# The passes of two matmul layers issued in turn, one by one instead of three by three

## The chip, the cores and the metric

The kernel runs on one core of a Trainium2 chip. The metric is the device time of one execution in microseconds (us), median over several runs. The core's engines are TensorE (PE, with its weight loads shown as PEld), VectorE (DVE), ScalarE (ACT), GpSimd (POOL) and SyncE (SP), which issues the transfers. Matmul results go to PSUM, eight banks of 128 partitions by 2 KB, where they are added up; ScalarE and VectorE read them out.

## The reference

The computation is an attention over channels followed by a two-layer network with the exact GELU, for 4 batches of 6080 tokens with 256 channels:

```python
qn = q / (norm(q, axis=1) + 1e-6); kn = k / (norm(k, axis=1) + 1e-6)
a = softmax(kn.transpose(0, 2, 1) @ qn / tau)      # 256 x 256 per batch
x = (v @ a).reshape(24320, 256)
h = x @ w_in                                       # 256 -> 2048
g = 0.5 * h * (1 + erf(h / sqrt(2)))
out = g @ w_out                                    # 2048 -> 256
```

## The kernel before, in words

The attention matrix is folded into the first layer's weights, so per batch one pair of weight matrices is left: tokens times 256x2048, GELU, times 2048x256. Precision is kept by splitting every operand into a high and a low part; a product of two operands is then three matmul passes (high by high, high by low, low by high) that add up in one PSUM bank.

The tokens of a batch are cut into 6 pairs of blocks (two blocks of 512 tokens each, the last pair of 480), the 2048 hidden channels into 8 slices. One slice of one pair is called a **unit** here; there are 4 x 6 x 8 = 192. In all but the first pair a unit's first layer is computed as a Strassen-like scheme of seven **products** (`first_products`, called P0 to P6 here), each of three passes (L458, L459, L460, called p1, p2, p3). They go into three banks. Bank *one* takes P0, P2, P4 and P6 in turn, added up: between them the partial sum is read out, after P0 and P2 by a copy on ScalarE (`kept`, L491), after P4 by an addition on VectorE (`added`, L496, which also follows P3 and P5). So P2 can't begin before the copy after P0 is done, nor P4 before the copy after P2, nor P6 before the addition after P4. Four blocks come out; each goes through GELU twice on ScalarE (`gh`, rounded, L466, and `g`, L467) and a subtraction on VectorE (`gl`, L468). The first pair uses eight plain products per unit instead.

The second layer of a unit is eight **groups** (`second_products`, called G0 to G7 here), each of three passes (L541, L542, L543, called s1, s2, s3; s1 and s3 read `gh`, s2 reads `gl`) into one of four other banks, which add up over the eight units of a pair. G0 and G1 read the first block made, G2 and G3 the last one made (out of P6). At a pair's end the four banks are copied out (L547 on ScalarE, L549 on VectorE).

`second_products` is a generator. The loop over the units runs the second layer one unit behind the first: while the products of a unit are written, the groups of the unit before are drawn in between, one group after each product, and the rest (G6's partner G7) at the unit's end. So TensorE gets three passes of a product, three of a group, and so on; a unit is 45 passes. Between units stand bursts of the next batch's scores (L191, L193) and, at a batch's end, the products that make the next batch's weights (L376 to L378).

The written order is not the last word: the framework that builds the program lists each engine's instructions itself, by its own estimate of when operands will be there, and keeps to the written order where it sees no reason to depart from it. Each engine then works through its list in order.

Of the kernel before, what the change touches and what calls it, by code (L numbers as in the profile page):

```python
# [60 lines left out]
def channel_attention_gelu_ffn(ctx, tc, qk, kqt, vt, tau, w_in, w_out, out):  # L61
# [38 lines left out]
    state = {}  # L100
# [3 lines left out]
    @contextmanager  # L104
    def behind(*names):
        with ExitStack() as stack:
            for name in names:
                stack.enter_context(tc.issue_after(marks[name].ins))
            yield
# [243 lines left out]
    def w_slot(g, i):  # L353
        if i != A21:
            return whs[g][:, i], wls[g][:, i]
        if g // 2 not in w21:
            w21[g // 2] = [pv.tile([P, 2, 2, P], F32R, name=f"v{x}{T2 + g // 2}") for x in "hl"]
        return [t[:, g % 2] for t in w21[g // 2]]
# [76 lines left out]
    def v_split(b, p, i):  # L435
        n = PAIRS[p][1]
        x = v_blocks(b, p)
        src = {B11: x[0, 0], B21: x[1, 0], B22: x[1, 1]}.get(i)
        if (b, p, i) == (0, 0, B12):
            src = x[0, 1]  # L440
        if src is None:
            src = vts[b, p][i - T1][:, :n]
        hi = pv.tile([P, NT], F32R, name=f"vh{i}")
        lo = pv.tile([P, NT], F32R, name=f"vl{i}")
        nc.scalar.copy(out=hi[:, :n], in_=src)
        nc.vector.tensor_tensor(out=lo[:, :n], in0=src, in1=f32(hi[:, :n]), op=ALU.subtract)
        vops[b, p, i] = hi, lo
# [5 lines left out]
    def product(b, p, u, a, v, ps, start, stop):  # L453
        n = PAIRS[p][1]
        g, q = divmod(u, 2)
        hi, lo = vops[b, p, v]
        wh, wl = (t[:, q] for t in w_slot(g, a))
        nc.tensor.matmul(ps[:, :n], wh, hi[:, :n], start=start, stop=False, skip_group_check=True)  # L458
        nc.tensor.matmul(ps[:, :n], wh, lo[:, :n], start=False, stop=False, skip_group_check=True)  # L459
        marks["product"] = nc.tensor.matmul(ps[:, :n], wl, hi[:, :n], start=False, stop=stop, skip_group_check=True)  # L460

    def gelu(src, n):
# [65 lines left out]
    def second_products(b, p, u, blocks):  # L528

        t0, n = PAIRS[p]  # L530
        wo = wos.pop((b, p, u))
        for j in range(2):
            for i in (1, 0):
                gh, gl = blocks[i, j]
                for c in range(NCT):
                    if u == 0 and i == 1:
                        po[j, c] = ps_o.tile([P, NT], F32, name="po")
                    o = po[j, c][:, :n]
                    cs = slice(c * P, (c + 1) * P)
                    first, last = u == 0 and i == 1, u == NU - 1 and i == 0  # L540
                    nc.tensor.matmul(o, wo[:, 0, i, cs], gh[:, :n], start=first, stop=False)  # L541
                    nc.tensor.matmul(o, wo[:, 0, i, cs], gl[:, :n], start=False, stop=False)  # L542
                    nc.tensor.matmul(o, wo[:, 1, i, cs], gh[:, :n], start=False, stop=last)  # L543
                    if last:
                        if c == 0:
                            osb = pg.tile([P, NCT, NT], F32, name="osb", bufs=2)
                            nc.scalar.copy(out=osb[:, 0, :n], in_=o)  # L547
                        else:
                            nc.vector.tensor_copy(out=osb[:, 1, :n], in_=o)  # L549
                            t = b * N + t0 + j * n  # L550
                            dst = out[:, t:t + n].rearrange("(t p) n -> p t n", p=P)
                            step = 1 if (b, p) == (B - 1, NP - 1) else NCT
                            for h in range(0, NCT, step):
                                nc.sync.dma_start(out=dst[:, h:h + step], in_=osb[:, h:h + step, :n])
                    yield
# [151 lines left out]
            w_group(b + 1, (w - 42) // 2)  # L707

    steps = [(b, p, u) for b in range(B) for p in range(NP) for u in range(NU)]
    second = iter(())  # L710
    for b, p, u in steps:
        pair = (b, p + 1) if p + 1 < NP else (b + 1, 0)
        products = plain_products if (b, p) == (0, 0) else first_products
        for i, _ in enumerate(products(b, p, u)):
            next(second, None)
            if u == NU - 1 and pair[0] < B and i < 6:
                v_split(*pair, ORDER[i][1])
        if u == NU - 1 and pair[0] < B:
            v_split(*pair, ORDER[6][1])
        for _ in second:  # L720
            pass
        if (b, p) == (0, 0):
            for _ in range(paces[u] if u < len(paces) else 0):
                with behind(*(["gelu"] if u == 0 else [])):
                    narrow_unit()
                if units:
                    load_unit()
        extras(b, p, u)
        second = second_products(b, p, u, state.pop("blocks"))
    for _ in second:  # L730
        pass

# [27 lines left out]
```

## Time and profile before

| what | value |
| --- | --- |
| median of 3 runs | 2187.51 us (2186.54 to 2188.09) |
| the profiled execution's own time | 2186.54 us |
| span of its instructions | 2184.8 us |
| TensorE busy | 2173.9 us |
| ScalarE busy | 1433.4 us (66%) |
| VectorE busy | 1391.2 us (64%) |

TensorE's busy time counts overlapping matmuls once; a matmul's recorded duration (0.39 us for 512 columns) runs into the next one's, so that the pace is read from the distance of two starts. The profiled execution is 1.74 us longer than its span and 0.97 us under the median.

### The profile page before, as it was taken

What the parts mean: (1) busy time and instruction counts of PE and PEld (TensorE: products, weight loads), DVE (VectorE), ACT (ScalarE), POOL (GpSimd) and SP (SyncE); (2) the same over time, 40 slices, a digit from 0 to 9 for tenths busy, and PEclk for the clock granted to TensorE, in tenths of its full rate; (3) what the DMA queues carried; (4) which work ended last, traced back from release to release, by engine and by line L of the source; (5) the groups of instructions that cost most, each with busy time, mean ns of one, the idle gap of its engine ahead of it and who ended that gap; (6) DMA issues with size and microseconds to landing.
All of it is one profiled execution on the core that took longest, in us unless ns stands there. A gap on an engine that the chain in (4) does not pass through costs nothing.

```text
span 2184.8 us, 26184 instructions
## 1 busy us (share of the span) xinstructions
PE 2173.9 (100%) x9664; PEld 1794.0 (82%) x9664; DVE 1391.2 (64%) x2179; ACT 1433.4 (66%) x2595; POOL 1.3 (0%) x8
## 2 busy tenths in 40 slices
PE   8999999999999999999999999999999999999999
PEld 7788888888888888888888888888888888888888
DVE  6995767656677575675667757657467555555554
ACT  6666666667566676676765666767576566666665
POOL 0000000000000000000000000000000000000000
PEclk9999999999999999999999999999999999999999
DMA  9552544422343343542323335343132122121121
GB/s 381 195 207 104 174 135 158 160 87 87 106 144 106 121 168 116 174 157 64 106 97 133 116 116 174 134 155 126 49 114 97 58 87 72 64 97 66 68 78 47
DMA packets 77056, 267.52 MB, mean 122 GB/s; under 512 B 7680, under 2 KB 9728, under 8 KB 74880
## 3 DMA queue, kind: packets, MB, share of 16 engines
q1 hardware_dynamic: 76928, 265.84, 35.3%
q8 instruction: 76, 1.25, 0.2%
q14 instruction: 52, 0.43, 0.1%
HBM read 232.52 MB, written 33.29 MB: 122 GB/s over the span
## 4 chain that ended last, share of the span: by engine, by line
PE 98%; DVE 1%; DMA 0%; ACT 0%; issue 0%; SPq 0%; ACTq 0%; DVEq 0%
PE po L543 16%; PE po L541 16%; PE po L542 16%; PE ph L460 14%; PE ph L459 14%; PE ph L458 14%; PE ph L191 3%; PE ph L149 2%; PE ph L193 1%; PE ph L378 1%; PE ph L376 1%; PE ph L377 1%; DMA raw<-qk 0%; DVE nt L243 0%; PE po L172 0%
## 5 line engine op out<-in xcount | busy, mean ns | idle before, releaser
L468 DVE TENSOR_TENSOR gl<-g,gh 128x512 fp32r<-128x512 f32 (+1 forms) x768 | 522.1, 682 | 145.9 <-ACT g L467 142.1
L543 PE MATMUL po<-gh,wo 128*128 128x512 f32 (+1 forms) x1536 | 605.4, 394 | 0.0
L541 PE MATMUL po<-gh,wo 128*128 128x512 f32 (+1 forms) x1536 | 599.3, 390 | 1.0 <-ACT gh L466 1.0
L542 PE MATMUL po<-gl,wo 128*128 128x512 f32 (+1 forms) x1536 | 596.0, 388 | 0.0
L496 DVE TENSOR_TENSOR h<-ph,p 128x512 f32<-128x512 f32 (+1 forms) x368 | 251.7, 684 | 534.2 <-PE ph L460 438.9
L460 PE MATMUL ph<-vh,wl 128*128 128x512 f32 (+1 forms) x1336 | 523.0, 391 | 0.0
L459 PE MATMUL ph<-vl,wh 128*128 128x512 f32 (+1 forms) x1336 | 521.7, 391 | 0.0
L458 PE MATMUL ph<-vh,wh 128*128 128x512 f32 (+1 forms) x1336 | 520.7, 390 | 0.2 <-ACT wh L362 0.2
L466 ACT ACTIVATE gh<-h 128x512 fp32r<-128x512 f32 (+1 forms) x552 | 345.1, 625 | 243.1 <-DVE h L496 238.4
L491 ACT COPY p<-ph 128x512 f32<-128x512 f32 (+1 forms) x368 | 213.3, 583 | 263.2 <-PE ph L460 262.9
L542 PEld LDWEIGHTS po<-gl,wo 128*128 128x128 f32 x1536 | 288.5, 188 | 63.9
L541 PEld LDWEIGHTS po<-gh,wo 128*128 128x128 f32 x1536 | 288.5, 188 | 62.6 <-ACT gh L466 1.5
L543 PEld LDWEIGHTS po<-gh,wo 128*128 128x128 f32 x1536 | 288.5, 188 | 61.3
L467 ACT ACTIVATE g<-h 128x512 f32<-128x512 f32 (+1 forms) x552 | 337.4, 611 | 0.0
L459 PEld LDWEIGHTS ph<-vl,wh 128*128 128x128 f32 x1336 | 251.3, 188 | 56.6
L458 PEld LDWEIGHTS ph<-vh,wh 128*128 128x128 f32 x1336 | 251.2, 188 | 54.0 <-DVE h L496 3.1
L460 PEld LDWEIGHTS ph<-vh,wl 128*128 128x128 f32 x1336 | 251.1, 188 | 50.6
L491 ACT COPY u<-ph 128x512 f32<-128x512 f32 (+1 forms) x184 | 106.7, 580 | 111.8 <-PE ph L460 111.8
L466 ACT ACTIVATE gh<-ph 128x512 fp32r<-128x512 f32 (+1 forms) x216 | 125.1, 579 | 23.6 <-PE ph L460 19.4
L467 ACT ACTIVATE g<-ph 128x512 f32<-128x512 f32 (+1 forms) x216 | 126.4, 586 | 1.6 <-DVE gl L468 1.5
L496 DVE TENSOR_TENSOR h<-ph,u 128x512 f32<-128x512 f32 (+1 forms) x184 | 125.4, 681 | 2.7
L209 ACT ACTIVATE kqc<-kqc 128x1024 f32<-128x1024 f32 x72 | 76.4, 1061 | 35.6 <-DMA kqc<-kqt 35.1
(135 smaller groups left out, 1351.4 us busy)
## 6 DMA issues: line engine op xcount, KB each, us to landing
wo<-keep_out SPq DMA_DIRECT2D x184, 512.0 KB, 3.3
raw<-qk SPq DMA_DIRECT2D x95, 512.0 KB, 4.2
kqc<-kqt SPq DMA_DIRECT2D x72, 512.0 KB, 4.4
v_raw<-vt SPq DMA_DIRECT2D x20, 1024.0 KB, 5.6
out<-osb SPq DMA_DIRECT2D x40, 512.0 KB, 3.4
win<-keep_in SPq DMA_DIRECT2D x12, 1024.0 KB, 4.8
keep_in<-win SPq DMA_DIRECT2D x4, 1024.0 KB, 4.6
keep_out<-wo SPq DMA_DIRECT2D x8, 512.0 KB, 3.8
```

The source lines that it names most:

```text
L209: nc.scalar.activation(out=x, in_=x, func=AF.Square, accum_out=state["nsum"][:, t, c:c + 1])
L458: nc.tensor.matmul(ps[:, :n], wh, hi[:, :n], start=start, stop=False, skip_group_check=True)
L459: nc.tensor.matmul(ps[:, :n], wh, lo[:, :n], start=False, stop=False, skip_group_check=True)
L460: marks["product"] = nc.tensor.matmul(ps[:, :n], wl, hi[:, :n], start=False, stop=stop, skip_group_check=True)
L466: nc.scalar.activation(out=gh[:, :n], in_=src, func=AF.Gelu)
L467: marks["gelu"] = nc.scalar.activation(out=g[:, :n], in_=src, func=AF.Gelu)
L468: nc.vector.tensor_tensor(out=gl[:, :n], in0=g[:, :n], in1=f32(gh[:, :n]), op=ALU.subtract)
L491: nc.scalar.copy(out=t[:, :n], in_=ps[:, :n])
L496: nc.vector.tensor_tensor(out=h[:, :n], in0=ps[:, :n], in1=t[:, :n], op=ALU.add)
L541: nc.tensor.matmul(o, wo[:, 0, i, cs], gh[:, :n], start=first, stop=False)
L542: nc.tensor.matmul(o, wo[:, 0, i, cs], gl[:, :n], start=False, stop=False)
L543: nc.tensor.matmul(o, wo[:, 1, i, cs], gh[:, :n], start=False, stop=last)
```

## The change

The generator now yields after every pass instead of after every group, and `product` draws one pass of the second layer after its first and after its second pass; the loop draws the third. The number of passes, their operands and the banks are the same. TensorE's row becomes p1 s1 p2 s2 p3 s3, and at a unit's end, behind P6, the last pass of G6 and the three of G7 are left, where it was both groups whole.

```diff
--- before.py
+++ after.py
@@ -456,7 +456,9 @@
         hi, lo = vops[b, p, v]
         wh, wl = (t[:, q] for t in w_slot(g, a))
         nc.tensor.matmul(ps[:, :n], wh, hi[:, :n], start=start, stop=False, skip_group_check=True)
+        next(state["second"], None)
         nc.tensor.matmul(ps[:, :n], wh, lo[:, :n], start=False, stop=False, skip_group_check=True)
+        next(state["second"], None)
         marks["product"] = nc.tensor.matmul(ps[:, :n], wl, hi[:, :n], start=False, stop=stop, skip_group_check=True)
 
     def gelu(src, n):
@@ -539,7 +541,9 @@
                     cs = slice(c * P, (c + 1) * P)
                     first, last = u == 0 and i == 1, u == NU - 1 and i == 0
                     nc.tensor.matmul(o, wo[:, 0, i, cs], gh[:, :n], start=first, stop=False)
+                    yield
                     nc.tensor.matmul(o, wo[:, 0, i, cs], gl[:, :n], start=False, stop=False)
+                    yield
                     nc.tensor.matmul(o, wo[:, 1, i, cs], gh[:, :n], start=False, stop=last)
                     if last:
                         if c == 0:
@@ -707,7 +711,7 @@
             w_group(b + 1, (w - 42) // 2)
 
     steps = [(b, p, u) for b in range(B) for p in range(NP) for u in range(NU)]
-    second = iter(())
+    second = state["second"] = iter(())
     for b, p, u in steps:
         pair = (b, p + 1) if p + 1 < NP else (b + 1, 0)
         products = plain_products if (b, p) == (0, 0) else first_products
@@ -726,7 +730,7 @@
                 if units:
                     load_unit()
         extras(b, p, u)
-        second = second_products(b, p, u, state.pop("blocks"))
+        second = state["second"] = second_products(b, p, u, state.pop("blocks"))
     for _ in second:
         pass
```

The first place is TensorE in an ordinary unit, at the start of the unit: `ph` is the bank of a product, `po` that of a group, `vh`/`vl` and `wh`/`wl` the high and low parts of tokens and weights. Lines after the first edit are two or four higher in the new file (L460 to L462 for p2 and p3; L543, L545, L547 for s1, s2, s3). Before:

```order
L458 MATMUL ph<-vh_8009,wh_506 128x512
L459 MATMUL ph<-vl_8010,wh_506 128x512
L460 MATMUL ph<-vh_8009,wl_507 128x512
L541 MATMUL po<-gh,wo 128x512
L542 MATMUL po<-gl,wo 128x512
L543 MATMUL po<-gh,wo 128x512
L458 MATMUL ph<-vh_8022,wh_506 128x512
L459 MATMUL ph<-vl_8023,wh_506 128x512
```

After the change:

```order
L458 MATMUL ph<-vh_8009,wh_506 128x512
L543 MATMUL po<-gh,wo 128x512
L460 MATMUL ph<-vl_8010,wh_506 128x512
L545 MATMUL po<-gl,wo 128x512
L462 MATMUL ph<-vh_8009,wl_507 128x512
L547 MATMUL po<-gh,wo 128x512
L458 MATMUL ph<-vh_8022,wh_506 128x512
L543 MATMUL po<-gh,wo 128x512
```

The last pass of a product moved two places back (from third to fifth of the six), the first pass of a group two places ahead (from fourth to second), the second pass of a group one place ahead.

The second place is TensorE in a unit that opens a pair, from the group behind P5 to the unit's end; the L458 row here is the first pass of P6. Before:

```order
L541 MATMUL po<-gh,wo 128x512
L542 MATMUL po<-gl,wo 128x512
L543 MATMUL po<-gh,wo 128x512
L458 MATMUL ph<-vh_2211,wh_81 128x512
L459 MATMUL ph<-vl_2212,wh_81 128x512
L460 MATMUL ph<-vh_2211,wl_82 128x512
L541 MATMUL po<-gh,wo 128x512
L542 MATMUL po<-gl,wo 128x512
L543 MATMUL po<-gh,wo 128x512
L541 MATMUL po<-gh,wo 128x512
```

After the change (the rows begin with the last passes of P5 and its group):

```order
L545 MATMUL po<-gl,wo 128x512
L462 MATMUL ph<-vh_2198,wl_82 128x512
L547 MATMUL po<-gh,wo 128x512
L543 MATMUL po<-gh,wo 128x512
L545 MATMUL po<-gl,wo 128x512
L458 MATMUL ph<-vh_2213,wh_81 128x512
L460 MATMUL ph<-vl_2214,wh_81 128x512
L462 MATMUL ph<-vh_2213,wl_82 128x512
L547 MATMUL po<-gh,wo 128x512
L543 MATMUL po<-gh,wo 128x512
```

Here the list departs from the written order: P6 begins two places later than the rule of turns would have it, behind two passes of G6, and its three passes stand together; its last pass is where the rule of turns would put it.

The third place is VectorE in the same unit, from the addition after P3 to the addition after P5; the addition after P4 is the second L496 (L498 after), which P6 waits for. `vs` makes sums for the next pair's tokens, `osb` is the copy of a finished output bank. Before:

```order
L496 TENSOR_TENSOR h<-ph,p_2254 128x512
L427 TENSOR_TENSOR vs_2742<-v_raw 128x512
L549 COPY osb<-po 128x512
L468 TENSOR_TENSOR gl<-g,gh 128x512
L496 TENSOR_TENSOR h<-ph,p_2263 128x512
L496 TENSOR_TENSOR h<-ph,u_2271 128x512
```

After the change:

```order
L498 TENSOR_TENSOR h<-ph,p_2256 128x512
L553 COPY osb<-po 128x512
L427 TENSOR_TENSOR vs_2742<-v_raw 128x512
L470 TENSOR_TENSOR gl<-g,gh 128x512
L498 TENSOR_TENSOR h<-ph,p_2265 128x512
L498 TENSOR_TENSOR h<-ph,u_2273 128x512
```

The copy of the output bank and the sum for the next pair changed places; `gl` still stands ahead of the addition after P4.

## Rows read from the trace of the kernel before

**Rows 1.** The page, engines and granted clock: busy time of each engine (share of the span, instructions), and the clock that TensorE was granted in 40 equal slices of the span, in tenths of full speed.

```profile
PE 2173.9 (100%) x9664; PEld 1794.0 (82%) x9664; DVE 1391.2 (64%) x2179; ACT 1433.4 (66%) x2595; POOL 1.3 (0%) x8
...
PEclk9999999999999999999999999999999999999999
```

**Rows 2.** The page, chain that ended last: shares of the span by engine.

```profile
PE 98%; DVE 1%; DMA 0%; ACT 0%; issue 0%; SPq 0%; ACTq 0%; DVEq 0%
```

**Rows 3.** The view of waits, whole span: who waited for whom, us in total, times, longest us.

```profile
PEld ph L458 <- DVE h L496: 3.1, 9, 0.3
...
PE po L541 <- ACT gh L466: 1.0, 1, 1.0
...
PE ph L458 <- ACT wh L362: 0.2, 1, 0.2
```

**Rows 4.** Timeline of TensorE in an ordinary unit, products four and five and the groups behind them, up to the first pass of product six. Columns: start, duration, engine, line, operation. The durations of matmuls overlap; the starts are what is read.

```profile
1005.21 0.39 PE L458 MATMUL ph<-vh,wh 128*128 128x512 f32 x1
1005.43 0.39 PE L459 MATMUL ph<-vl,wh 128*128 128x512 f32 x1
1005.66 0.39 PE L460 MATMUL ph<-vh,wl 128*128 128x512 f32 x1
1005.89 0.39 PE L541 MATMUL po<-gh,wo 128*128 128x512 f32 x1
1006.12 0.39 PE L542 MATMUL po<-gl,wo 128*128 128x512 f32 x1
1006.35 0.40 PE L543 MATMUL po<-gh,wo 128*128 128x512 f32 x1
1006.59 0.39 PE L458 MATMUL ph<-vh,wh 128*128 128x512 f32 x1
...
1007.97 0.39 PE L458 MATMUL ph<-vh,wh 128*128 128x512 f32 x1
```

**Rows 5.** Timeline of TensorE: twelve passes of 512 columns of a weight product (L376 to L378, six into one bank, six into the next), first pass and the pass after the twelfth; and sixteen passes of a score burst (L191 and L193, 512 and 256 columns, all into one bank), first pass and the pass after the sixteenth.

```profile
590.95 0.39 PE L376 MATMUL ph<-win,eh 128*128 128x512 f32 x1
...
593.72 0.38 PE L458 MATMUL ph<-vh,wh 128*128 128x480 f32 x1
...
1010.04 0.40 PE L191 MATMUL ph<-hl 128*128 128x512 f32 x1
...
1012.82 0.39 PE L458 MATMUL ph<-vh,wh 128*128 128x512 f32 x1
```

**Rows 6.** Timeline, the same ordinary unit: the last pass of product two, the copy of its bank on ScalarE, and the addition on VectorE that empties the bank of product four.

```profile
1002.90 0.39 PE L460 MATMUL ph<-vh,wl 128*128 128x512 f32 x1
...
1003.33 0.59 ACT L491 COPY u<-ph 128x512 f32<-128x512 f32 x1 [0.79 <-PE ph L460]
...
1006.15 0.69 DVE L496 TENSOR_TENSOR h<-ph,p 128x512 f32<-128x512 f32 x1 [0.69 <-ACT gh L466]
```

**Rows 7.** Timeline of the first unit after a unit that opened a pair: the two instructions that make the high and low parts of the last block (gh on ScalarE, gl on VectorE), and the two passes that read them first, one unit later.

```profile
254.99 0.58 ACT L466 ACTIVATE gh<-ph 128x512 fp32r<-128x512 f32 x1
...
256.49 0.68 DVE L468 TENSOR_TENSOR gl<-g,gh 128x512 fp32r<-128x512 f32 x1
...
258.57 0.39 PE L541 MATMUL po<-gh,wo 128*128 128x512 f32 x1
...
258.80 0.39 PE L542 MATMUL po<-gl,wo 128*128 128x512 f32 x1
```

**Rows 8.** Timeline of a unit that opens a pair, from the last pass of product three to the first weight load of product six.

```profile
249.15 0.40 PE L460 MATMUL ph<-vh,wl 128*128 128x512 f32 x1
...
249.65 0.69 DVE L496 TENSOR_TENSOR h<-ph,p 128x512 f32<-128x512 f32 x1 [0.43 <-ACT osb L547]
...
250.26 0.69 DVE L427 TENSOR_TENSOR vs<-v_raw 128x512 f32<-128x512 f32 x1
...
250.38 0.64 ACT L466 ACTIVATE gh<-h 128x512 fp32r<-128x512 f32 x1 [0.72 <-DVE h L496]
...
250.86 0.68 DVE L549 COPY osb<-po 128x512 f32<-128x512 f32 x1
...
250.91 0.62 ACT L467 ACTIVATE g<-h 128x512 f32<-128x512 f32 x1
...
251.57 0.69 DVE L468 TENSOR_TENSOR gl<-g,gh 128x512 fp32r<-128x512 f32 x1
...
252.18 0.68 DVE L496 TENSOR_TENSOR h<-ph,p 128x512 f32<-128x512 f32 x1
...
252.91 0.19 PEld L458 LDWEIGHTS ph<-vh,wh 128*128 128x128 f32 x1 [0.35 <-DVE h L496]
```

**Rows 9.** Timeline of the units that close a batch, the first and the last of three: the addition that empties the bank of product four, and the first pass of product six.

```profile
601.70 0.65 DVE L496 TENSOR_TENSOR h<-ph,p 128x480 f32<-128x480 f32 x1
...
602.60 0.38 PE L458 MATMUL ph<-vh,wh 128*128 128x480 f32 x1
...
1678.37 0.65 DVE L496 TENSOR_TENSOR h<-ph,p 128x480 f32<-128x480 f32 x1
...
1679.28 0.37 PE L458 MATMUL ph<-vh,wh 128*128 128x480 f32 x1
```

**Rows 10.** Timeline of the units that open the fifth pair of the second and third batch, the two of them: two copies of banks in a row on ScalarE, of which the first is that of product zero, and the first pass of product two.

```profile
967.65 1.07 ACT L491 COPY p<-ph 128x512 f32<-128x512 f32 x2
...
968.53 0.39 PE L458 MATMUL ph<-vh,wh 128*128 128x512 f32 x1
...
1506.01 1.07 ACT L491 COPY p<-ph 128x512 f32<-128x512 f32 x2
...
1506.89 0.39 PE L458 MATMUL ph<-vh,wh 128*128 128x512 f32 x1
```

## The prediction

> **What bounds the kernel now.** I read the page's engine shares and its chain first, then the waits, then TensorE's timeline. TensorE is busy all the time while ScalarE and VectorE have a third of the span free, and the granted clock is full, the 2.4 GHz level, in every slice [rows 1]. The chain that ended last is 98% TensorE [rows 2]. So the time is TensorE's passes times their distance, plus what TensorE waits. In the second layer's part it hardly waits: one wait of 1.0 us for `gh` and one of 0.2 us near the start, and nine weight loads of P6 that came late because VectorE's addition had not emptied the bank, 3.1 us of weight-load idle together [rows 3]. The distance of passes is read from an ordinary unit: twelve passes of 512 columns from 1005.21 to 1007.97, 2.76 us, 0.23 each [rows 4]. Whatever the change does to the time, it does to this distance or to a wait.
>
> **The work itself: 0.** No pass, operand, transfer or instruction of ScalarE or VectorE is added or removed. A unit has 45 passes before and after. What is new is that nearly every pass goes to another PSUM bank than the one ahead of it: before, the bank changed 15 times in a unit's 45 passes, now 43 times (42 in the alternating part and once into G7), 28 more in each of 184 units, 5152 in all. The trace has no strictly alternating stretch of this kind, so I bound the price of a bank change from both sides. In the ordinary unit the two changes at a product's end and a group's end took 0.23 and 0.24 us, the four distances inside 0.22, 0.23, 0.23 and 0.23 [rows 4]: means of 0.235 and 0.2275, so a change costs at most 0.0075 us, 5152 x 0.0075 = +39 us. Against it stand the twelve passes of a weight product, 590.95 to 593.72 = 2.77 us with two bank changes, where twelve ordinary ones took 2.76 with four [rows 4, 5]: a change then gains 0.005 us, 5152 x 0.005 = -26 us. Both ends are made of the last digit of the rows. The longest row decides: a score burst puts 8 x (512 + 256) = 6144 columns into one bank in 1012.82 - 1010.04 = 2.78 us, and the twelve ordinary passes, also 6144 columns, took 2.76 with four changes [rows 4, 5]. Columns set the distance, banks don't. I take 0 and keep both ends.
>
> **The waits that the change moves.** In one turn of six passes the last pass of a product goes from third to fifth place, so whatever empties its bank starts 2 x 0.23 = 0.46 us later, while the next product into that bank begins where it did. The first pass of a group comes 0.46 us sooner, the second 0.23 sooner. So the cover of each wait shrinks, and I go through them.
>
> *P2, P4 and P6 in ordinary units.* The last pass of P2 began at 1002.90, the copy ran from 1003.33 to 1003.92 [rows 6], P4 began at 1005.21 [rows 4]: 1.29 us to spare, 0.83 after. P2 has the same form (copy after P0). For P6, the addition ran from 1006.15 to 1006.84 [rows 6] and P6 began at 1007.97 [rows 4]: 1.13 us, 0.67 after. A release needs about 0.05 us to reach TensorE (addition ended 252.86, weight load 252.91 [rows 8]). All covered, cost 0; without this cover every unit would pay.
>
> The Trainium skill speaks against the change here: "Perfetto Trace Analysis", section "Matmuls", wants independent groups to rotate through PSUM banks so that the emptying of one overlaps the matmuls of the next, and an alternating order keeps each bank open for five places where it was three. Going by it a loss appears only where the overlap runs out, and with 0.67 us left it does not; the trace agrees so far.
>
> *Groups that read the last block.* P6's last pass is two places later and G2's first two sooner, so `gh` loses 0.92 us, `gl` 0.69. In the unit after a pair's opening, `gh` was ready at 255.57 and read at 258.57, `gl` ready at 257.17 and read at 258.80 [rows 7]: 3.00 and 1.63 us, 2.08 and 0.94 after. Cost 0. G0 reads the first block made, which is half a unit older.
>
> *Units that open a pair.* Here the nine late weight loads stand. VectorE has an output copy, a sum for the next pair and `gl` ahead of the addition that P6 waits for, and the chain is: P3's last pass 249.15, addition 249.65, `gh` 250.38, `g` 250.91, `gl` 251.57, addition 252.18 to 252.86, P6's load 252.91 [rows 8]. P3's last pass moves 0.46 us back, and the chain with it. But the new list of TensorE also begins P6 two places later, behind two passes of G6, as the second place in the order shows: another 0.46 us, the other way. The wait stays what it is, cost 0. Without that, 9 x 0.46 = 4.1 us.
>
> *Units that close a batch.* Three units, where P6 already stood behind G6 and two passes of G7 and does so still. The addition ended 602.35 and 1679.02, P6 began 602.60 and 1679.28 [rows 9]: 0.25 us to spare, 0.20 after the 0.05 of the release. The passes have 480 columns, two of them take 0.46 x 480/512 = 0.43. Cost 3 x 0.23 = 0.7 us.
>
> *P2 in two pair-opening units.* The copy of P0's bank came late on ScalarE: two copies in 1.07 us from 967.65, the first done at about 968.2, P2 at 968.53 [rows 10], some 0.3 to spare, 0.25 less the release. Short by 0.2, twice: 0.4 us.
>
> **Sum.** 0 + 0.7 + 0.4 = 1.1 us on the profiled execution's own 2186.5 us (span 2184.8 and 1.7 around it): 2187.6. That execution lies 1.0 us under the median of the runs shown, so against the median I say 2188.6 us. This is no change: about 0.2% (4.4 us) is what a measurement of this kernel can tell, so "same" means 2183.1 to 2191.9.
>
> **The rivals.**
> - *Slower: the pair openings pay after all.* VectorE's new list puts the output copy ahead of the sum for the next pair, and both still stand ahead of `gl`, behind which P6's addition waits. `g` would be done 0.46 later than 250.91 + 0.62 = 251.53, at 251.99; the copy and the sum began 0.60 and 0.71 us ahead of their followers [rows 8], so the mechanism decides from the point where the copy begins later than 251.99 - 1.31 = 250.68, and the copy can't begin before the last pass of G3 is through. It began at 250.86 behind the sum [rows 8]. If it costs up to 0.46 in nine units, 4.1 + 1.1 = 5.2: 2192.7. For it: these are the tightest spots in the kernel. Against it: ahead of the sum the copy should start sooner.
> - *Slower: a bank change has a price*, up to +39 us: 2227, the middle of the range 2208. For it only 0.01 us of rounding, against it the burst.
> - *Faster: a bank change gains* 0.005 us: 2188.6 - 26 = 2163. The same evidence, the other way.
> - *Much faster: the passes drop to their columns.* At the granted 2.4 GHz level 512 columns are 0.213 us and the rows show 0.23 [rows 1, 4]. If the 0.017 came from turning back into the same bank and went, 184 x 45 passes x 0.017 = 141 us: 2048. Against it: passes that do change the bank show the same 0.23 to 0.24 [rows 4].
>
> On that last rival the Trainium skill has a page: "TensorE: Matmul & The Clock Gate", section "Back-to-back issue gap", gives columns/2.4 + 2.5 ns, an estimate of 0.216 us for 512 columns; the trace does not agree, with 0.23 in every bank pattern shown, and by the page's figure the gain would be 8280 x 0.014 = 116 us (estimate).
>
> **How the numbers follow.** Forecast (waits covered, distance unchanged) 0.68; pair openings pay 0.14; a bank change costs 0.08; it gains 0.08; passes drop to their columns 0.02. Faster by over 0.2%: 0.10; slower: the second and third, 0.22; within: 0.68. The forecast's own range is 2185 to 2192. For 8 in 10 I let out the bank rivals and take in the pair openings with some room: 2183 to 2198.
>
> **What the new profile would show.** The distance of two starts in an ordinary unit stays 0.23, twelve passes 2.76. In the waits, the weight loads of P6 behind VectorE's addition stay near nine with a total of about 3 us, three more with about 0.2 each at the batch ends; if they grow to 7 us, the first rival is right. TensorE's wait for `gl` and `gh` stays empty beyond the start. I am wrong if the distance of passes moved in the third decimal (twelve passes other than 2.76), or if a wait shows up that the old trace had covered by over 0.6 us.

## The result, and the profile after

The changed kernel takes 2199.31 us (median of 6 runs, 2197.75 to 2201.49); the kernel before, on the same chips, 2187.68 us (6 runs, 2186.54 to 2188.09). The ratio is 1.0053 with a 95% interval of 1.0043 to 1.0063: 11.6 us, 0.5%, slower. The forecast was no change, 2188.6.

The page of the changed kernel, engines, granted clock and shares of the chain:

```profile
span 2197.4 us, 26017 instructions
...
PE 2185.4 (99%) x9664; PEld 1794.1 (82%) x9664; DVE 1391.0 (63%) x2179; ACT 1439.5 (66%) x2595; POOL 1.3 (0%) x8
...
PEclk9999999999999999999999999999999999999999
...
PE 95%; DVE 2%; DMA 1%; ACT 1%; issue 0%; SPq 0%; DVEq 0%; ACTq 0%
```

The span grew by 12.6 us (2184.8 before), TensorE's busy time by 11.5 with the same number of instructions, and the clock is still full [rows 1]. So most of the loss is inside what the page calls busy. The chain lost three points on TensorE to VectorE, a transfer and ScalarE [rows 2]: there are new waits as well. The two are measured apart.

**The distance of two passes.** Three units of the second pair, 135 passes of 512 columns without a wait or a burst between them. Timeline of TensorE, first pass of the first and first pass after the third (start, duration). Before:

```profile
179.57 0.39 PE L458 MATMUL ph<-vh,wh 128*128 128x512 f32 x1
...
210.65 0.39 PE L458 MATMUL ph<-vh,wh 128*128 128x512 f32 x1
```

After the change:

```profile
182.82 0.39 PE L458 MATMUL ph<-vh,wh 128*128 128x512 f32 x1
...
214.04 0.39 PE L458 MATMUL ph<-vh,wh 128*128 128x512 f32 x1
```

31.08 us became 31.22: 0.2302 us a pass became 0.2313, 0.047 us a unit. Over the whole trace the mean distance of the second layer's part went from 0.23037 to 0.23129 us for 512 columns (some 7150 distances) and from 0.21662 to 0.21746 for 480 (1416): 7150 x 0.00092 + 1416 x 0.00084 = 7.8 us.

**The waits.** The view of waits after (who, for whom, us in total, times, longest):

```profile
PEld ph L458 <- DVE h L498: 5.0, 10, 2.1
...
DVE vs L427 <- DMA v_raw<-vt: 3.2, 2, 1.8
...
PEld po L543 <- ACT gh L468: 2.3, 2, 1.5
...
PE ph L458 <- DVE h L498: 1.7, 1, 1.7
...
PE po L543 <- ACT gh L468: 1.5, 2, 1.0
PEld ph L458 <- ACT u L493: 1.3, 5, 0.3
...
PEld po L545 <- DVE gl L470: 0.5, 1, 0.5
```

Beside [rows 3]: the late weight loads of P6 are ten where they were nine, and the tenth alone has 2.1 us; there is a second wait for `gh`, and small ones behind the copies of `u` and for `gl`. Where the distance of two starts is over 0.25 us (0.24 for 480 columns), I add up what is above 0.232 (0.220) and call that the wait of TensorE: 5.5 us before, 9.2 after. These sums, and those of the runs below, take in 1.6 to 1.9 us that lie ahead of the first product, in the preparation of the first batch; from the first product on it is 3.8 before and 7.3 after, so 3.5 more.

The largest stands in the unit that opens the second pair. VectorE there, before:

```profile
162.56 0.69 DVE L496 TENSOR_TENSOR h<-ph,p 128x512 f32<-128x512 f32 x1
163.17 0.68 DVE L468 TENSOR_TENSOR gl<-g,gh 128x512 fp32r<-128x512 f32 x1
163.77 0.68 DVE L427 TENSOR_TENSOR vs<-v_raw 128x512 f32<-128x512 f32 x1
```

VectorE and TensorE in the same unit after the change:

```profile
163.44 0.68 DVE L553 COPY osb<-po 128x512 f32<-128x512 f32 x1
165.96 0.69 DVE L427 TENSOR_TENSOR vs<-v_raw 128x512 f32<-128x512 f32 x1 [1.84 <-DMA v_raw<-vt]
166.57 0.68 DVE L470 TENSOR_TENSOR gl<-g,gh 128x512 fp32r<-128x512 f32 x1
167.17 0.68 DVE L498 TENSOR_TENSOR h<-ph,p 128x512 f32<-128x512 f32 x1
...
165.81 0.40 PE L545 MATMUL po<-gl,wo 128*128 128x512 f32 x1
167.91 0.50 PE L458 MATMUL ph<-vh,wh 128*128 128x512 f32 x1 [1.70 <-DVE h L498]
```

Before, the sum for the next pair (L427) stood behind the addition that P6 waits for. After, it stands ahead of it, behind the output copy, and waits 1.84 us for the tokens of the next pair. Two things met: the new place in VectorE's list, and a transfer that took 7.3 us to land where it took 5.4; why it took longer is not shown. The views of transfers, the issue in 100 to 170 us (before, then after):

```profile
v_raw<-vt SPq DMA_DIRECT2D x1, 1024.0 KB, 5.4
```

```profile
v_raw<-vt SPq DMA_DIRECT2D x1, 1024.0 KB, 7.3
```

P6 starts 1.97 us late there. The second largest is a group that reads the last block made, early in the fifth pair of the second batch. ScalarE and TensorE, after the change:

```profile
993.46 1.28 ACT L305 ACT_TABLE_LOAD   x1
994.76 0.20 ACT L305 ACTIVATE small<-small 128x4 f32<-128x4 f32 x1
994.98 1.28 ACT L468 ACT_TABLE_LOAD   x1
...
998.37 0.57 ACT L468 ACTIVATE gh<-ph 128x512 fp32r<-128x512 f32 x1
...
999.00 0.50 PE L543 MATMUL po<-gh,wo 128*128 128x512 f32 x1 [0.45 <-ACT gh L468]
```

A small operation of the next batch's softmax brings two loads of a table, 2.56 us, ahead of the block's `gh`. They stood there before too (from 985.92 and 987.44), covered; the group, now 0.46 us earlier against its block's last pass 0.46 later, waits 0.72 us in all (two starts). The rest: 0.13 us each in three units where P4 waits for the copy after P2, 0.05 to 0.07 at the three batch ends, 0.3 for `gl` in the last unit. The nine pair openings of before wait 0.15 us each, where it was 0.18.

Account of the 12.6 us: 7.8 distance of passes, 3.5 waits from the first product on, 1.0 ahead of it (it began at 64.35 instead of 63.39; in the traces of the other full kernels below it lies anywhere from 62.6 to 64.4, so this part is no mark of the change); 0.3 is not located.

### The profile page after: what moved, and what is told of

Same layout as the page of the kernel before. It is cut to its first block, busy times and chain, and to the rows that moved or that the text cites. A ratio compares the mean times of both kernels' runs of the same rounds, so it can differ in the third digit from the quotient of the medians.

```text
span 2197.4 us, 26017 instructions
## 1 busy us (share of the span) xinstructions
PE 2185.4 (99%) x9664; PEld 1794.1 (82%) x9664; DVE 1391.0 (63%) x2179; ACT 1439.5 (66%) x2595; POOL 1.3 (0%) x8
## 4 chain that ended last, share of the span: by engine, by line
PE 95%; DVE 2%; DMA 1%; ACT 1%; issue 0%; SPq 0%; DVEq 0%; ACTq 0%
PE po L543 16%; PE po L545 16%; PE po L547 16%; PE ph L458 14%; PE ph L460 14%; PE ph L462 14%; PE ph L191 3%; PE ph L193 1%; DMA raw<-qk 1%; DMA v_raw<-vt 1%; DVE acc L139 1%; PE ph L376 1%; PE ph L378 1%; PE ph L377 1%; DVE gl L470 0%
## 5 line engine op out<-in xcount | busy, mean ns | idle before, releaser
L498 DVE TENSOR_TENSOR h<-ph,p 128x512 f32<-128x512 f32 (+1 forms) x368 | 251.6, 684 | 568.9 <-PE ph L462 433.6
L543 PE MATMUL po<-gh,wo 128*128 128x512 f32 (+1 forms) x1536 | 602.5, 392 | 1.5 <-ACT gh L468 1.5
L545 PE MATMUL po<-gl,wo 128*128 128x512 f32 (+1 forms) x1536 | 601.0, 391 | 0.1
L547 PE MATMUL po<-gh,wo 128*128 128x512 f32 (+1 forms) x1536 | 600.9, 391 | 0.0
L458 PE MATMUL ph<-vh,wh 128*128 128x512 f32 (+1 forms) x1336 | 522.5, 391 | 1.9 <-DVE h L498 1.7
L460 PE MATMUL ph<-vl,wh 128*128 128x512 f32 (+1 forms) x1336 | 522.3, 391 | 0.0
L462 PE MATMUL ph<-vh,wl 128*128 128x512 f32 (+1 forms) x1336 | 521.4, 390 | 0.0
L545 PEld LDWEIGHTS po<-gl,wo 128*128 128x128 f32 x1536 | 288.7, 188 | 65.1 <-DVE gl L470 0.5
L543 PEld LDWEIGHTS po<-gh,wo 128*128 128x128 f32 x1536 | 288.3, 188 | 64.2 <-ACT gh L468 2.3
L547 PEld LDWEIGHTS po<-gh,wo 128*128 128x128 f32 x1536 | 288.6, 188 | 63.4
L458 PEld LDWEIGHTS ph<-vh,wh 128*128 128x128 f32 x1336 | 250.9, 188 | 61.7 <-DVE h L498 5.0
L462 PEld LDWEIGHTS ph<-vh,wl 128*128 128x128 f32 x1336 | 251.1, 188 | 54.6
L460 PEld LDWEIGHTS ph<-vl,wh 128*128 128x128 f32 x1336 | 251.0, 188 | 52.6
L498 DVE TENSOR_TENSOR h<-ph,u 128x512 f32<-128x512 f32 (+1 forms) x184 | 125.7, 683 | 4.5
L191 PE MATMUL ph<-hl 128*128 128x512 f32 x272 | 96.2, 393 | 0.0
```

What stands on the lines that cost most here:

```text
L191: nc.tensor.matmul(s, hl[:, 0, j, 0, cs], hl[:, :, j, 1], start=(i == 0), stop=False, skip_group_check=True)
L498: nc.vector.tensor_tensor(out=h[:, :n], in0=ps[:, :n], in1=t[:, :n], op=ALU.add)
```

## The experiments

The waits could be read off the trace; why the same passes stand further apart could not. The theories, by the letters of the expectations: **A**, a change of PSUM bank has a price; **B**, a change of the weight tile has one; **E**, what the other engines read and write at that time holds TensorE up; **D**, the start addresses of a pass's two operands in SBUF, the on-chip memory that it reads them from, set its distance (**D2** is its second form: the address of the moving tile against that of the weight tile, and the order in which such differences follow one another); **F**, addresses set the distance, VectorE's list sets the waits, and the two add. What another letter stands for is said where it is used.

**1. TensorE alone.** Nine stretches of 480 passes on fixed tiles; the whole computation is left out, so its time means nothing. Among them (bank, weight tile, moving tile of each pass): one of each; banks in turn; weight tiles in turn; the row of before; the row of after.

```diff
+    seq = steps([(a, wh, vh)])
...
+    seq = steps([(a, wh, vh), (b, wh, vh)])
...
+    seq = steps([(a, wh, vh), (a, wl, vh)])
...
+    seq = steps([(a, wh, vh), (a, wh, vl), (a, wl, vh), (b, wo, gh), (b, wo, gl), (b, wp, gh)])
...
+    seq = steps([(a, wh, vh), (b, wo, gh), (a, wh, vl), (b, wo, gl), (a, wl, vh), (b, wp, gh)])
```

> Leaves out the whole computation: nine stretches of 480 passes of 512 columns on TensorE alone, nothing else running, results of no use. Stretches in order: one bank, one weight tile, one moving tile; two banks in turn; two weight tiles in turn; both in turn; two moving tiles in turn; then the row of before (three into one bank, three into the other), the row of after (one by one), two-two-one-one, and three by three with the weights changed at every pass. In the changed kernel the mean distance of two 512-column passes is 0.2313 us where it was 0.2304. Theory A (a change of PSUM bank costs, about 0.0014 us each): second and fourth stretch 0.0014 above the first, the row of after 0.0009 above the row of before, two-two-one-one halfway. Theory B (a change of the weight tile costs): third and fourth stretch above the first and second, rows of after and the last stretch 0.0009 above the row of before, two-two-one-one like before. Theory C (TensorE by itself doesn't care; the difference comes from the other engines' traffic or from the chip): all rows the same within 0.0002.

The view of one line: first and last start of the row three by three, and of the row one by one.

```profile
L69 PE MATMUL a<-vh,wh x80: 389/389/389, 553.8 to 661.2; 128*128 128x512 f32 x80
...
L69 PE MATMUL b<-gh,wp x80: 389/389/389, 554.9 to 662.4; 128*128 128x512 f32 x80
```

```profile
L73 PE MATMUL a<-vh,wh x80: 389/389/389, 662.6 to 770.0; 128*128 128x512 f32 x80
...
L73 PE MATMUL b<-gh,wp x80: 389/389/389, 663.7 to 771.2; 128*128 128x512 f32 x80
```

(662.4 - 553.8) / 479 = 0.2267 and (771.2 - 662.6) / 479 = 0.2267. All nine stretches stand at 0.22667 us (the first once its opening passes are through), whatever bank, weight tile or order. A and B fall as properties of TensorE by itself, and there was a second surprise: neither kernel reaches 0.22667.

**2. Two, two, one, one.** The change with one `next` and one `yield` fewer, so that TensorE gets p1 p2 s1 s2 p3 s3.

```diff
         nc.tensor.matmul(ps[:, :n], wh, hi[:, :n], start=start, stop=False, skip_group_check=True)
-        next(state["second"], None)
         nc.tensor.matmul(ps[:, :n], wh, lo[:, :n], start=False, stop=False, skip_group_check=True)
         next(state["second"], None)
...
                     nc.tensor.matmul(o, wo[:, 0, i, cs], gh[:, :n], start=first, stop=False)
-                    yield
                     nc.tensor.matmul(o, wo[:, 0, i, cs], gl[:, :n], start=False, stop=False)
                     yield
```

> Row of TensorE p1 p2 s1 s2 p3 s3: four bank changes in six passes where before has two and the changed kernel six; the two pairs with the same weight tile stand together as before. Theory A: half of the growth of the distance, mean 0.2308, 4 us from it, about 2192 with none of the large waits, 2194 with them. Theory B: distance 0.2304 as before, 2188 to 2190. Theory C: distance as before or anywhere, without relation to the row.

2200.21 us, ratio 1.0057 (1.0044 to 1.0069). The three units take 31.22 us: all of the longer distance with four changes of bank in six passes, where the change has six and the kernel before two. The waits are 8.3 us. That is no price per change of bank.

**3. Weight tiles in the order high, low, high,** in the kernel before:

```diff
-        nc.tensor.matmul(ps[:, :n], wh, lo[:, :n], start=False, stop=False, skip_group_check=True)
-        marks["product"] = nc.tensor.matmul(ps[:, :n], wl, hi[:, :n], start=False, stop=stop, skip_group_check=True)
+        nc.tensor.matmul(ps[:, :n], wl, hi[:, :n], start=False, stop=False, skip_group_check=True)
+        marks["product"] = nc.tensor.matmul(ps[:, :n], wh, lo[:, :n], start=False, stop=stop, skip_group_check=True)
```

and the same in the groups.

> Before, with the three passes of each product and group in the order high-high, low-high, high-low, so that the weight tile changes at every pass, as in the changed kernel, and the bank changes twice in six passes as before. Theory A: distance 0.2304, 2187.7 as before. Theory B: distance 0.2313, 8 us more, 2196. Theory C: 2187.7.

2186.1 us, ratio 0.9993 (0.9984 to 1.0002), three units in 31.08: B falls in the kernel too.

**4. The sum held back.** The changed kernel, with VectorE's sum for the next pair told to stand behind the block's subtraction:

```diff
-        nc.vector.tensor_tensor(out=gl[:, :n], in0=g[:, :n], in1=f32(gh[:, :n]), op=ALU.subtract)
+        marks["gl"] = nc.vector.tensor_tensor(out=gl[:, :n], in0=g[:, :n], in1=f32(gh[:, :n]), op=ALU.subtract)
...
-                v_sums(*pair, u - 4)
+                with behind("gl"):
+                    v_sums(*pair, u - 4)
```

> The changed kernel with the sums for the next pair's tokens (L427 to L433) held behind the gl that is written ahead of them, so that none stands ahead of the addition that P6 waits for. All theories: the 1.9 us wait at the opening of the second pair goes, and the nine late weight loads of P6 shrink from about 0.16 us to none, together 3 to 3.5 us: 2196. Theories A and B: the distance stays 0.2313, so that 8 us over before remain. Theory C: the distance may come out as before.

2194.43 us, ratio 1.0030 (1.0019 to 1.0042). VectorE at the opening of the second pair:

```profile
162.49 0.68 DVE L553 COPY osb<-po 128x512 f32<-128x512 f32 x1
163.27 0.69 DVE L498 TENSOR_TENSOR h<-ph,p 128x512 f32<-128x512 f32 x1
163.88 0.68 DVE L470 TENSOR_TENSOR gl<-g,gh 128x512 fp32r<-128x512 f32 x1
```

The addition follows the copy at once, although this transfer took 7.4 us to land. The waits fall from 9.2 to 4.7 us, below those of before, and the time by 4.9; the three units stay at 31.22. So the two halves of the loss are independent, and the distance is the larger.

**5. The start addresses.** TensorE alone again (the whole computation is left out), 19 stretches of 240 passes at chosen addresses. In the kernels the tokens' tiles begin 192 bytes, the blocks' (`gh`, `gl`) 64 and the weight tiles 128 bytes past a multiple of 512 (read from the built program; no view of the profile has it). All tiles of run 1 began at 128. `tiles` takes the places of tokens, blocks and weight tiles, `single` those of one moving and one weight tile; L74 is the row of before, L78 that of after.

```diff
+    seq = [before(tiles(192, 64, 128))[i % len(before(tiles(192, 64, 128)))] for i in range(REPS)]
...
+    seq = [after(tiles(192, 64, 128))[i % len(after(tiles(192, 64, 128)))] for i in range(REPS)]
...
+    seq = [single(64, 0)[i % len(single(64, 0))] for i in range(REPS)]
```

> Leaves out the whole computation: stretches of 240 passes of 512 columns on TensorE alone, with chosen start addresses of the operands in SBUF, results of no use. In the kernel the moving tiles of the first layer start 192 bytes, those of the second 64 bytes past a multiple of 512, the weight tiles 128; in the run with TensorE alone all started at multiples of 128, and the distance was 0.22667 us in every row of passes. Theory D (a moving tile that starts off a multiple of 128 bytes makes TensorE's pass longer, and by how much hangs on which tiles follow each other): rows of before and after with the kernel's addresses 0.2300 and 0.2311, both 0.2267 with everything at multiples of 512; single tile at 64 or 192 bytes above 0.2267. Theory E (other engines' reads of SBUF and PSUM lengthen the passes): 0.2267 in every stretch, at any address.

The view of one line, first and last start; L98, L102, L106 and L110 are one moving tile 0, 64, 128 and 192 bytes past the weight tile's place:

```profile
L74 PE MATMUL a<-arena x120: 390/392/399, 67.0 to 121.3; 128*128 128x512 f32 x120
...
L74 PE MATMUL b<-arena x120: 388/392/398, 67.7 to 122.0; 128*128 128x512 f32 x120
...
L78 PE MATMUL a<-arena x120: 388/391/398, 122.2 to 177.2; 128*128 128x512 f32 x120
...
L78 PE MATMUL b<-arena x120: 390/393/399, 122.5 to 177.5; 128*128 128x512 f32 x120
...
L98 PE MATMUL a<-arena x240: 389/389/395, 399.6 to 453.8; 128*128 128x512 f32 x120
...
L102 PE MATMUL a<-arena x240: 388/392/397, 454.0 to 508.7; 128*128 128x512 f32 x120
...
L106 PE MATMUL a<-arena x240: 390/393/404, 508.9 to 564.5; 128*128 128x512 f32 x120
...
L110 PE MATMUL a<-arena x240: 392/393/398, 564.7 to 620.5; 128*128 128x512 f32 x120
```

At the kernel's addresses, (122.0 - 67.0) / 239 = 0.2301 and (177.5 - 122.2) / 239 = 0.2314 us (the last 160 starts, past the first ones: 0.22998 and 0.23114): the distances of the two real kernels, with no other engine at work; the row of run 2 stands at 0.2310 (L82). E falls, and an order does matter. At 0 for all tiles both orders stand at 0.22667. What counts is the moving tile's start less the weight tile's, modulo 256 bytes: 0 gives 0.2267 us, 64 gives 0.2289, 128 gives 0.2323, 192 gives 0.2333; both at 64 give 0.2267 again, so D as first put (multiples of 128 are fast) is wrong. Two other starts: 32 bytes 0.2333, 4 bytes 0.2367.

**6 and 7. All tiles of the second layer's part moved by 64 bytes,** in the kernel before and in the changed one. The differences are now 128 (tokens) and 0 (blocks).

```diff
+    ptau.tile([P, 16], F32, name="pad")
...
-    pwh.tile([P, 16], F32, name="pad")
```

> Before, with 64 bytes of unused space ahead of the tokens' tiles and without the 64 bytes ahead of the weight tiles, so that all moving tiles start at multiples of 128 bytes and the weight tiles where they were. Theory D: the distance falls from 0.2304 to 0.2267, 8664 x 0.0037 = 32 us less, 2156. Theory E: 2187.7 as before.

> The changed kernel with the same 64 bytes moved. Theory D: the distance falls from 0.2313 to 0.2267 as well, so that what is left between it and the aligned kernel of before are the waits alone, 4 us: 2160. Theory E: 2199 as the changed kernel.

Three by three: 2199.48 us, ratio 1.0055 (1.0043 to 1.0068), three units in 31.32. One by one: 2188.89, ratio 1.0004 (0.9995 to 1.0013), three units in 31.06. Both expectations missed, as they rest on D's first form. The sign has turned: at these addresses the order of the change has the shorter distance, by 0.26 us in three units, and wins 10.6 us over the other in spite of 9.2 us of waits against 5.1. The order is not slow; it was slow at these addresses.

**8. The order by itself.** TensorE alone (the whole computation is left out): one weight tile, two moving tiles at differences of 64 and 192, in runs of 1, 2, 3, 6 and 24, in one bank and in two banks in turn, and the rows of runs 6 and 7.

```diff
+    def runs(p, q, k):
+        w = cut(8, 128, P)
+        return [(a, w, cut(0, p, NT))] * k + [(a, w, cut(4, q, NT))] * k
```

> Leaves out the whole computation: stretches of 240 passes on TensorE alone at chosen addresses, results of no use. Theory D2, from the run before: a pass is longer by what the start of its moving tile lies past the start of the weight tile that is loaded under it, modulo 256 bytes: 0 gives 0.2267 us, 64 0.2289, 128 0.2323, 192 0.2333, and the order of the differences decides too. Two moving tiles at 192 and 64, one weight tile at 128, all into one bank: one by one 0.2311, three by three 0.2300, long runs the mean of 0.2289 and 0.2333, 0.2311. The same with two banks in turn: no different. Everything at 128: 0.2267 in every row. Theory A: with one bank throughout no difference between one by one and three by three, and 0.0014 for each change with two.

One bank in runs of 1 (L84), 2 (L89) and 3 (L94), then two banks in runs of 1 (L109) and 3 (L114):

```profile
L84 PE MATMUL a<-arena x240: 388/393/399, 66.7 to 121.9; 128*128 128x512 f32 x120
...
L89 PE MATMUL a<-arena x240: 388/391/392, 122.1 to 176.7; 128*128 128x512 f32 x120
...
L94 PE MATMUL a<-arena x240: 388/392/398, 176.9 to 231.9; 128*128 128x512 f32 x120
...
L109 PE MATMUL a<-arena x120: 388/391/398, 342.9 to 397.9; 128*128 128x512 f32 x120
...
L109 PE MATMUL b<-arena x120: 390/393/399, 343.1 to 398.1; 128*128 128x512 f32 x120
...
L114 PE MATMUL a<-arena x120: 390/392/394, 398.4 to 452.7; 128*128 128x512 f32 x120
...
L114 PE MATMUL b<-arena x120: 388/392/398, 399.1 to 453.3; 128*128 128x512 f32 x120
```

Runs of 1: (121.9 - 66.7) / 239 = 0.2310; of 2: 0.2285 (0.2283 past the first starts); of 3: 0.2301; longer ones 0.2305 to 0.2312. With two banks the distances are the same to the fourth digit (past the first starts 0.2311 and 0.2300 either way). So the bank has no part in it; the order of the address differences has. One by one is here the mean of the two single values (0.2289 and 0.2333); for 128 and 0 in turn it is not (0.2300, with 0.2323 and 0.2267 alone). The rows of runs 6 and 7 give 0.2322 and 0.2300, what those kernels show, and with all tiles at equal places 0.22667 in either order. D2 holds.

**9 and 10. All moving tiles put at the weight tiles' place** (128 past a multiple of 256), in the kernel before and in the changed one, by pads alone:

```diff
+    pv.tile([P, 48], F32, name="pad")
...
+    pg.tile([P, 32], F32, name="pad", bufs=1)
...
-    pwh.tile([P, 16], F32, name="pad")
```

> Before, with unused space ahead of the tokens' tiles (192 bytes) and ahead of the GELU's tiles (128 bytes) and the 64 bytes ahead of the weight tiles taken away, so that the moving tiles of both layers and all weight tiles start at 128 modulo 256. Theory D2: distance 0.2267 in place of 0.2304, 8664 x 0.0037 = 32 us less: 2156, some us more if the faster TensorE meets new waits. Theory A: 2188.

> The changed kernel with the same addresses. Theory D2: distance 0.2267 as well, so the order no longer matters to it, and what remains over the run beside it are the waits, 4 to 6 us: 2160 to 2162. Theory A: the distance stays 0.0009 above that of the run beside it, 8 us more: 2168.

Three by three: 2165.4 us, ratio 0.9899 (0.9884 to 0.9914). One by one: 2170.48, ratio 0.9923 (0.9910 to 0.9935). Three units take 30.60 us in both, 0.2267 a pass. The order has no price left, and the 5 us between the two are waits, 7.8 against 13.5: with the passes closer together, the waits at pair openings grow.

Both expectations missed: run 9 gained 22 us and not 32. They had counted all 8664 passes at 0.0037 us, and the 1433 of 480 columns, in the last pair of each batch, gained nothing: that is 5 of the missing 10 us, and longer waits in run 9 are another 2.3. Three units of 480 columns, first pass of the first and first pass after the third, before, then run 9:

```profile
2108.96 0.38 PE L458 MATMUL ph<-vh,wh 128*128 128x480 f32 x1
...
2138.20 0.38 PE L458 MATMUL ph<-vh,wh 128*128 128x480 f32 x1
```

```profile
2089.80 0.38 PE L459 MATMUL ph<-vh,wh 128*128 128x480 f32 x1
...
2119.05 0.38 PE L459 MATMUL ph<-vh,wh 128*128 128x480 f32 x1
```

That is 29.24 and 29.25 us, 0.2166 and 0.2167 a pass. Three such units take 29.46 us on average in the changed kernel and 29.09 in run 7, whose tiles do not match: at 480 columns equal places are not the fastest ones seen.

**11 and 12. The same two with the sum held back** as in run 4.

> The start addresses of the ninth run (moving and weight tiles all 128 bytes past a multiple of 256), the order three by three, and VectorE's sum for the next pair told to stand behind the block's subtraction (gl), as in the fourth run. Theory F (addresses set the distance, and VectorE's list sets the waits; the two add): the distance stays 0.2272 us, and of the 7.8 us that TensorE waited between passes in the ninth run's trace some 2 to 4 go, since its pair openings waited 0.3 to 0.5 us each: 2161 to 2164 us. Rival (the sum only moves the wait to another instruction of VectorE): 2165 us, as in the ninth run.

> The start addresses of the tenth run, the order one by one, and the sum for the next pair behind the block's subtraction. Theory F (the 5 us between the ninth and the tenth run are waits of the same kind as those that the fourth run took out): the distance stays 0.2272 us, the 13.5 us of waiting in the tenth run's trace fall by 4 to 6, and the time is 2164 to 2167 us, level with the ninth run. Rival (the one-by-one order has waits of another kind, for gh and gl, that this does not touch): 2169 to 2171 us, as in the tenth run.

2162.93 us, ratio 0.9885 (0.9870 to 0.9900), and 2163.94, ratio 0.9887 (0.9871 to 0.9904). Both beat the kernel before by 1.1%, and now the change costs nothing that can be told. The waits are 3.9 and 5.3 us; the row of P6 behind VectorE's addition, 4.1 us in nine in run 9 and 3.1 in [rows 3], is gone from the view. F holds. Run 11, the same two passes as above:

```profile
178.48 0.39 PE L459 MATMUL ph<-vh,wh 128*128 128x512 f32 x1
...
209.08 0.39 PE L459 MATMUL ph<-vh,wh 128*128 128x512 f32 x1
```

All full kernels together (differences of address: moving tile less weight tile, modulo 256 bytes; three units: 135 passes of 512 columns). The kernel before, run again beside the later ones, took 2187.4 to 2188.5:

| kernel | order | tokens, blocks | three units, us | waits, us | median, us |
| --- | --- | --- | --- | --- | --- |
| before | 3 by 3 | 64, 192 | 31.08 | 5.5 | 2187.7 |
| after | 1 by 1 | 64, 192 | 31.22 | 9.2 | 2199.3 |
| run 2 | 2, 2, 1, 1 | 64, 192 | 31.22 | 8.3 | 2200.2 |
| run 3 | 3 by 3, high-low-high | 64, 192 | 31.08 | 4.6 | 2186.1 |
| run 4 | 1 by 1, sum held | 64, 192 | 31.22 | 4.7 | 2194.4 |
| run 6 | 3 by 3 | 128, 0 | 31.32 | 5.1 | 2199.5 |
| run 7 | 1 by 1 | 128, 0 | 31.06 | 9.2 | 2188.9 |
| run 9 | 3 by 3 | 0, 0 | 30.60 | 7.8 | 2165.4 |
| run 10 | 1 by 1 | 0, 0 | 30.60 | 13.5 | 2170.5 |
| run 11 | 3 by 3, sum held | 0, 0 | 30.60 | 3.9 | 2162.9 |
| run 12 | 1 by 1, sum held | 0, 0 | 30.60 | 5.3 | 2163.9 |

## Why the prediction was wrong, step by step

*The work itself: 0.* This is the step that failed. "Columns set the distance, banks don't" is right in its second half (run 8) and wrong in its first: at 512 columns the runs show 0.2267 to 0.2367 us, by the operands' start addresses and the order in which they come. The term measured 7.8 us. That lies inside the range kept for a price of the bank change (up to +39 us), but it is no such price: run 7 has the same changes of bank and no loss of distance. The reading was at fault too: the effect is 0.4%, 0.01 us in 2.76, which is the last digit of twelve passes [rows 4]; three units give the distance to the fourth digit. The score burst that decided [rows 5] has other tiles, at other places, and could not stand in for the row that the change makes.

*Rival "passes drop to their columns".* It saw that 0.23 us is more than the columns at the granted clock, and asked the right question, but put it down to the bank. The part that can be had is 0.2302 - 0.2267 = 0.0035 us a pass of 512 columns (runs 9 to 12), by addresses. By the Trainium skill, "TensorE: Matmul & The Clock Gate", section "Back-to-back issue gap", columns/2.4 + 2.5 ns is an estimate of 0.216 us; that section gives the formula for an isolated matmul, and 0.131 us for a stream of 512 columns, which the prediction did not say. The runs agree with neither: no stretch of 512 columns went below 0.2267.

*P2, P4 and P6 in ordinary units: 0.* Held, but for P4 in three units, 0.13 us each: the cover read from one ordinary unit [rows 6] was not the smallest.

*Groups that read the last block: 0.* Held but for one of them: 0.7 us where two table loads stand ahead of `gh`, and 0.3 us for `gl` in the last unit. The cover of 3.00 us [rows 7] was again that of one unit.

*Units that open a pair: 0.* Right for the nine that waited before: 0.15 us each, P6 two places later, as the order showed. Wrong for a tenth that had not waited: 1.97 us. The first rival named the mechanism, VectorE's new list ahead of the addition, but not the place nor the price; it watched when the output copy starts, and what came late was the tokens' transfer behind the sum. The third place of the order belongs to another opening, where the sum stood ahead of that addition before as well; in the opening that paid it stood behind it, and no row shown told so. But that place did show an instruction that waits for a transfer ahead of `gl` and the addition, and the prediction asked only for VectorE's time, not for the transfer's. Run 4 shows that this and its kin are worth 4.9 us.

*Units that close a batch, 0.7 us; P2, 0.4 us.* Over-sized: 0.05 to 0.07 us each for the three, and no wait of P2 over 0.05.

*The bet on what would show it.* Both of the conditions named for being wrong came true: the distance moved in the third decimal (0.2302 to 0.2313), and a wait appeared that the old trace had covered.

## What to carry to other kernels

Read the distance of passes over a hundred or more of them, compare it with the shortest that a bare loop of the same passes reaches on the chip, and if it is longer, look at the start addresses of moving and weight tiles before anything else: pads of a few hundred bytes were worth 1% here, more than any order. Do so at the number of columns that the kernel uses: equal places were the best seen for 512 columns and not for 480. A change of order that loses or wins a few tenths of a per cent without a wait to show for it may only be meeting such addresses, so try it at matched addresses before judging it. And when a list changes, ask of every instruction that comes to stand ahead of a critical one what it may wait for, transfers included, in every unit and not in the typical one.

## What the runs showed of the hardware that was not expected

A pass of 512 columns in the number format of these kernels (fp32r), with its own weight load, takes 0.2267 us at the least seen, and 0.2289, 0.2323 or 0.2333 us when the moving tile starts 64, 128 or 192 bytes past the weight tile's place modulo 256 (0.2367 at 4 bytes). At 480 columns equal places give 0.2167 us and a mix of 128 and 0, one by one, 0.2155 (run 7). Two differences in turn don't simply add: at 512 columns 64 and 192 give 0.2311 one by one, 0.2283 in runs of two, 0.2300 three by three; 128 and 0 give 0.2300 one by one and 0.2322 three by three. The bank does not change these values (run 8), nor does it matter whether one weight tile or several at equal places take part (runs 5 and 8). What in the chip makes them is not settled by these runs, and no rule for the mixed rows is offered.
